# Two maxima of head 1 moved into the first section of scores, two of head 0 taken out of the second

## The chip, the cores and the metric

The kernel runs on one core of a Trainium2 chip. The time is the device time of one execution in microseconds (us); the figure for a kernel is the median of several runs. All views of the profile come from one profiled execution. PE is TensorE, PEld its weight loads, DVE VectorE, ACT ScalarE, POOL GpSimd, SP SyncE (which here issues almost all DMAs).

## The reference

Two mixers of a sequence of 2048 rows by 512 columns are computed and mixed row by row with a gate.

```python
def reference(A_x, A_dft_seq_re, A_dft_seq_im, A_dft_hid_re, A_dft_hid_im, B_x, B_wqkv, B_wo, gate_w):
    x = A_x                                                # both mixers read A_x
    g = sigmoid((x * gate_w).sum(-1, keepdims=True))
    # mixer A: real part of a DFT over the hidden, then over the sequence dimension
    a = einsum("bsd,ed->bse", x, dft_hid_re)
    b = einsum("bsd,ed->bse", x, dft_hid_im)
    y = einsum("ts,bse->bte", dft_seq_re, a) - einsum("ts,bse->bte", dft_seq_im, b)
    # mixer B: softmax attention, 32 heads of 16 columns, no mask
    q, k, v = heads(x @ wqkv)
    p = softmax(einsum("bhqd,bhkd->bhqk", q, k) * 16 ** -0.5)
    o = merge(einsum("bhqk,bhkd->bhqd", p, v)) @ wo
    return g * y + (1 - g) * o
```

All is float32. The kernel splits factors into a high and a low part and adds three products for each.

## The kernel before, in words

**Stages.** From 0 to about 195 us the kernel makes q and k of all heads and writes them to DRAM (`qk_d`), then v and the imaginary part of the hidden DFT. From 195 us on one stream of PE work runs to the end. Into it are woven the DFT products (`d`, line 471), the scores with their exponentials (`s`, lines 800 and 801), the row maxima that the softmax needs ahead of the scores (`a`, matmul at line 294, maximum over 512 columns by DVE at line 296), and the products of the exponentials with v (`acc`, line 846).

**Heads and pairs.** The 32 heads go as 16 pairs; of each pair head 0 works on rows 0 to 63 of the PE array and head 1 on rows 64 to 127. A pair's q and k lie in `qs[p % 2]` and `ks[p % 2]`, so that two pairs have room. `load_stacks(p, [h])` (lines 267 to 281) fills the 64 rows of head h from DRAM: one or two DMAs of constants and six of 128 KB, by turns q (line 280) and k (line 281), all issued by SP. The last of the six is a `ks<-qk`. For pair p it is called for head 0 at unit 32(p - 1) and for head 1 two units later:

```python
    for p in range(1, NP):
        for h in range(2):
            at(32 * (p - 1) + 2 * h * (p > 1), load_stacks, p, [h])
```

A unit is 128 keys by 1024 queries of both heads; 32 units make a pair. The scores of pair p begin at unit 32p.

**Maxima.** A head's maxima are a stream of its own: tile i of head h belongs to pair i // 64 (`a_tile`, lines 288 to 301). 44 tiles of each head are done before 195 us (`LEAD`). When both heads have done 32 tiles of a half pair, `m_parts` and `m_rows` (lines 303 to 326) form the negated maxima and send them to two rows of `qs`.

**Segments.** What stands in which order is written out by hand, as strings. `segment(pattern, half, ds, stop)` (lines 954 to 1003) goes through the slots of one. A slot of one letter issues one DFT product on the 64 rows of `half`, and beside it one score (`s`) or one maximum (`a`) of the other head, `1 - half`, on the other 64 rows; the two run side by side. `-` is a DFT product with nothing beside it. Two letters (`sA`, `aS`) are a score or maximum of the other head beside one, in capitals, of the head on `half`, with no DFT product. `+s` and `+a` are a score or a maximum with nothing beside it. A digit names the PSUM bank; without one, scores take turns on banks 0 to 2 and maxima on banks 3 to 5. `|` takes the next unit's products with v.

The stream is: 12 full-height DFT products (`pump`), `START[0]` on half 0, 12 more, `START[1]` on half 1, two units' products with v; then 13 times the two segments of `THIN`, 96 times two segments of `FULL`, 13 times the two of `NINE`, and a tail. In `THIN` a segment serves the other head with 7 maxima and the own one with 1. In `FULL` a segment on half 0 has 8 maxima of head 1, and the next, on half 1, 8 of head 0. The last four maxima of a `FULL` segment stand in its slots `a6 a3 a4 a1`, the last slot before `|`.

```python
    FULL = "a5 s4 a2 s0 a3 s6 a5 s4 s1 s0 s2 a6 a3 a4 s5 a1 | |"
    START = "sA s aS - - a s - - a s - - a", "s a s a s a s a s a s a +s +a"
    THIN = ("a2S4 a1 s3 a0 s6 s2 a4 s3 s1 a6 a0 s5 a2 s4A3 | |",
```

Each engine takes its instructions in order; a matmul that waits for data holds up all PE work behind it. SP, too, issues its DMAs in order.

Of the kernel before, what the change touches and what calls it, by code (L numbers as in the profile page):

```python
# [31 lines left out]
def mix_kernel(ctx: ExitStack, tc: tile.TileContext, xa_t, xa, wqkv, w_hid, w_seq, wo, gate_w, out):  # L32
# [820 lines left out]
    def take(gen, n, whole=True):  # L853

        got = []
        while len(got) < n:
            x = next(gen, None)
            if x is None:
                break
            x[0].left -= 1  # L860
            got.append((*x, x[0].left == 0))
            if whole and got[-1][4]:
                break
        return got
# [8 lines left out]
    def pump(gen, n):  # L873
        for x in take(gen, n, False):
            issue(x, None)
# [45 lines left out]


    FULL = "a5 s4 a2 s0 a3 s6 a5 s4 s1 s0 s2 a6 a3 a4 s5 a1 | |"
    START = "sA s aS - - a s - - a s - - a", "s a s a s a s a s a s a +s +a"
    THIN = ("a2S4 a1 s3 a0 s6 s2 a4 s3 s1 a6 a0 s5 a2 s4A3 | |",
            "a2S4 a1 s3 a0 s6 s2 a4 s3 s1 a6 a0 s5 a2 s4A3 | |")
    NINE = ("a3 s0 s5 a4 a1 s6 s3 a0 a2 s5A4 | s5S1 a3A0 |",
# [20 lines left out]
    def values(close=False):  # L948
        nonlocal valued
        i = pv(valued, close)  # L950
        valued += 1
        return i
# [69 lines left out]
    ds = take(hid, 12)  # L1022
    segment(START[0], 0, ds, False)
    pump(hid, 12)
    segment(START[1], 1, ds, True)
    values()
# [114 lines left out]
```

## Time and profile before

| | |
|---|---|
| time, median of 3 runs | 1656.97 us (1656.69 to 1657.71) |
| the profiled execution | 1657.73 us, its span 1656.0 us |
| PE busy | 1648.4 us, 100% of the span |
| DVE busy | 1381.0 us, 83% |
| ACT busy | 1259.6 us, 76% |
| POOL busy | 654.0 us, 39% |
| granted PE clock | 0.999 |

Busy times count overlapping instructions of an engine once. The time lies 1.73 us above the span of the same execution: what lies around the span is not in the views. In the views that list instructions the first number is the start in us from the span's start and the second the duration in us; SPq is SP's queue of DMA issues. A busy PE can still be waiting at the array's input, since the ends of its matmuls are modelled, so that starts are the safer reading.

### The profile page before, as it was taken

To read this page: it belongs to the slowest core of one execution; us is meant where nothing else is said; L and a number is where in the kernel's file an instruction comes from. 1 tells how busy PE (TensorE), PEld (TensorE's weight loads), DVE (VectorE), ACT (ScalarE), POOL (GpSimd) and SP (SyncE) were. 2 spreads that over 40 slices of the span, in tenths; PEclk is the share of its full clock that TensorE was granted. 3 is DMA by queue.
4 is the path that set the end of the run, shared out by engine and by line. 5 is a ranking of instruction groups with operands and counts; after the bars stand their busy time and mean duration, and the time that the engine had idled before them with its cause. 6 is when DMAs were issued, how large, how long until landed. Compare 5 with 4: busy or idle time off the path is not lost.

```text
span 1656.0 us, 34484 instructions
## 1 busy us (share of the span) xinstructions
PE 1648.4 (100%) x13082; PEld 990.4 (60%) x13082; DVE 1381.0 (83%) x2362; ACT 1259.6 (76%) x2469; POOL 654.0 (39%) x619
## 2 busy tenths in 40 slices
PE   9999999999999999999999999999999999999998
PEld 7888765555555555555555555555555555544454
DVE  5439888888888888888888888888888888899954
ACT  5212388888888888888788887888888887889996
POOL 0202133443434455444343455544434455333330
PEclk9999999999999999999999999999999999999999
DMA  9973610514151443414157434315141535452014
GB/s 291 348 166 109 186 20 9 70 34 85 46 91 47 74 113 81 95 46 79 47 90 255 92 115 95 87 59 92 47 91 56 116 104 119 139 186 47 25 44 142
DMA packets 85246, 167.16 MB, mean 101 GB/s; under 512 B 22460, under 2 KB 22716, under 8 KB 81068
## 3 DMA queue, kind: packets, MB, share of 16 engines
q1 hardware_dynamic: 84648, 164.30, 39.8%
q8 instruction: 103, 1.69, 0.5%
q10 hardware_dynamic: 432, 0.66, 0.1%
q14 instruction: 63, 0.52, 0.1%
HBM read 109.67 MB, written 55.17 MB: 100 GB/s over the span
## 4 chain that ended last, share of the span: by engine, by line
PE 99%; DMA 0%; DVE 0%; DVEq 0%; ACT 0%; SPq 0%; issue 0%
PE acc L846 28%; PE a L294 22%; PE s L800 19%; PE d L471 12%; PE s L385 3%; PE acc L800 3%; PE acc L294 2%; PE s L417 1%; PE d L385 1%; PE acc L808 1%; PE a L111 1%; PE a L110 1%; PE s L111 1%; PE s L110 1%; PE a L109 1%; PE s L109 1%
## 5 line engine op out<-in xcount | busy, mean ns | idle before, releaser
L296 DVE TENSOR_REDUCE mx<-a 128x1 f32<-128x512 f32 x1808 | 1127.8, 683 | 157.5 <-PE a L294 107.5
L801 ACT ACTIVATE pt<-s 128x512 f32<-128x512 f32 x1792 | 943.9, 628 | 15.1 <-PE s L800 11.1
L294 PE MATMUL a<-ks,qs 64*128 64x512 f32 (+1 forms) x1808 | 673.0, 408 | 0.0
L471 PE MATMUL d<-xab,ch 64*128 64x512 f32 x2016 | 648.1, 396 | 0.0
L800 PE MATMUL s<-qs,ks 64*128 64x512 f32 (+1 forms) x1792 | 591.5, 399 | 0.0
L828 POOL TENSOR_TENSOR oe<-oe,part 128x512 f32<-128x512 f32 x215 | 278.1, 1293 | 659.3 <-ACT part L827 654.3
L846 PE MATMUL acc<-pt,vt 128*17 128x512 f32 x3968 | 479.0, 595 | 0.0
L294 PEld LDWEIGHTS a<-ks,qs 64*128 64x128 f32 (+1 forms) x1808 | 322.2, 184 | 242.6 <-issue 133.1
L471 PE MATMUL d<-xab,cl 64*128 64x512 f32 x1008 | 399.3, 396 | 0.0
L471 PEld LDWEIGHTS d<-xab,ch 64*128 64x128 f32 x2016 | 366.6, 184 | 14.2
L800 PEld LDWEIGHTS s<-qs,ks 64*128 64x128 f32 (+1 forms) x1792 | 320.3, 184 | 81.0 <-ACT pt L801 29.8
L827 ACT COPY part<-acc 128x512 f32<-128x512 f32 x215 | 126.3, 588 | 202.2 <-issue 187.1
L846 PEld LDWEIGHTS acc<-pt,vt 128*17 128x17 f32 x3968 | 89.0, 96 | 228.2 <-issue 148.4
L471 PEld LDWEIGHTS d<-xab,cl 64*128 64x128 f32 x1008 | 185.6, 184 | 6.9
L296 DVE TENSOR_REDUCE mx<-acc 128x1 f32<-128x512 f32 x240 | 165.5, 690 | 11.4
L456 POOL TENSOR_TENSOR cl<-craw,ch 128x512 fp32r<-128x512 f32 x126 | 162.1, 1287 | 10.1
L801 ACT ACTIVATE pt<-acc 128x512 f32<-128x512 f32 x244 | 148.1, 607 | 0.0
L800 PE MATMUL acc<-qs,ks 64*128 64x512 f32 (+1 forms) x244 | 95.4, 391 | 0.0
L294 PE MATMUL acc<-ks,qs 64*128 64x512 f32 (+1 forms) x240 | 94.1, 392 | 0.0
L455 POOL CAST ch<-craw 128x512 fp32r<-128x512 f32 x126 | 77.1, 612 | 18.5 <-PE d L471 14.2
L471 PE MATMUL d<-wre,xab 64*128 64x512 f32 x336 | 83.0, 392 | 0.0
L471 PE MATMUL d<-wo_hl,o_hl 64*128 64x512 f32 x252 | 66.7, 395 | 0.0
(175 smaller groups left out, 1199.4 us busy)
## 6 DMA issues: line engine op xcount, KB each, us to landing
craw<-w_seq SPq DMA_DIRECT2D x128, 256.0 KB
qk<-hl SPq DMA_DIRECT2D x32, 512.0 KB
qs<-qk SPq DMA_DIRECT2D x96, 128.0 KB
ks<-qk SPq DMA_DIRECT2D x96, 128.0 KB
b<-hl SPq DMA_DIRECT2D x16, 512.0 KB
xab<-b SPq DMA_DIRECT2D x16, 512.0 KB
o<-oe SPq DMA_DIRECT2D x62, 128.0 KB
oh<-nh SPq DMA_DIRECT2D x12, 512.0 KB
```

The lines of the kernel that those rows point to most:

```text
L109: nc.tensor.matmul(ps, sh, mh, start=first, stop=False)
L294: nc.tensor.matmul(ps, qs[p % 2][r, qt * P:(qt + 1) * P], ks[p % 2][r, kb * 512:(kb + 1) * 512], start=True, stop=True)
L296: user = nc.vector.tensor_reduce(mx[p % 2][:, h, qt, kb:kb + 1], ps, AX.X, ALU.max)
L385: i = nc.tensor.matmul(ps, st[r], mv[r], start=not half and not j, stop=half == 1 and j == 11)
L455: nc.gpsimd.tensor_copy(h1, raw)
L456: nc.gpsimd.tensor_tensor(l1, raw, h1.bitcast(F32), ALU.subtract)
L471: i = nc.tensor.matmul(self.ps, st[r], mv[r], start=not self.begun, stop=stop)
L800: nc.tensor.matmul(ps, ks[p % 2][rr, kt * P:(kt + 1) * P], qs[p % 2][rr, q0:q0 + 512], start=True, stop=True)
L801: return nc.scalar.activation(pts[u][:, 2 * qb + h], ps, AF.Exp, bias=0.0, scale=DH ** -0.5)
L827: nc.scalar.copy(part[0], acc)
L828: nc.gpsimd.tensor_tensor(total, total, part[0], ALU.add)
L846: i = nc.tensor.matmul(acc[32 * j:32 * j + 17], v[:, 16 * h:16 * h + 17], pt[:, j], start=begin, stop=done or close)
```

## The change

Only the two strings of `START` change.

```diff
-    START = "sA s aS - - a s - - a s - - a", "s a s a s a s a s a s a +s +a"
+    START = "sA s aS a - a s a - s a - - a", "s a s a s a s a s a s s"
```

The first section has 14 slots as before, with six maxima of head 1 where it had four (and one score a slot earlier). The second has 12 slots where it had 14, with five maxima of head 0 where it had seven; its last score stands beside the last DFT product. The counts of scores, of DFT products and of all maxima stay. What changes for good is where the two streams of maxima stand: behind the two sections head 0 was at tile 52 and head 1 at tile 48; now both are at 50. All later patterns are the same, so at every later slot for a maximum, head 1 takes the tile two further on than before and head 0 the tile two further back, to the end.

PE in the first section, where `qs_973` and `ks_975` are the buffers of pair 0 and `d` is the DFT product; one piece of the difference:

```order
 L800 MATMUL s<-qs_973,ks_975 128x512
 L471 MATMUL d<-wre_1450,xab_204 128x512
+L294 MATMUL a<-ks_975,qs_973 128x512
 L471 MATMUL d<-wre_1451,xab_204 128x512
 L471 MATMUL d<-wre_1455,xab_204 128x512
-L294 MATMUL a<-ks_975,qs_973 128x512
+L800 MATMUL s<-qs_973,ks_975 128x512
 L471 MATMUL d<-wre_1451,xab_204 128x512
-L800 MATMUL s<-qs_973,ks_975 128x512
+L294 MATMUL a<-ks_975,qs_973 128x512
 L471 MATMUL d<-wre_1452,xab_204 128x512
 L471 MATMUL d<-wre_1456,xab_204 128x512
```

A maximum now stands beside a product that had nothing beside it, and the score and the maximum behind it have moved up.

PE at the end of the second section, up to the products with v (`acc<-pt,vt`):

```order
 L800 MATMUL s<-qs_973,ks_975 128x512
 L471 MATMUL d<-wre_1452,xab_204 128x512
-L294 MATMUL a<-ks_975,qs_973 128x512
-L800 MATMUL s<-qs_973,ks_975 128x512
-L294 MATMUL a<-ks_975,qs_973 128x512
+L800 MATMUL s<-qs_973,ks_975 128x512
 L846 MATMUL acc<-pt,vt 17x512 x8
```

Two maxima of head 0 are gone, and no score or maximum is left without a partner.

PE at the end of one `FULL` segment on half 0, the one in which head 1 goes over to pair 6 in the changed kernel; before, with the semaphores that each instruction waits for (`qs_974`, `ks_976` hold pair 5, and `qs_973`, `ks_975` pair 6; DMAHW are those of SP's DMAs):

```order
L294 MATMUL a<-ks_976,qs_974 128x512 [waits DVE_49]
L471 MATMUL d<-xab_206,ch 128x512
L294 MATMUL a<-ks_976,qs_974 128x512 [waits Activation_49]
L471 MATMUL d<-xab_206,cl 128x512
L800 MATMUL s<-qs_974,ks_976 128x512 [waits DVE_49]
L471 MATMUL d<-xab_206,ch 128x512 x2
L294 MATMUL a<-ks_976,qs_974 128x512 [waits Activation_49]
L846 MATMUL acc<-pt,vt 17x512 [waits DVE_49]
```

and after:

```order
L294 MATMUL a<-ks_976,qs_974 128x512 [waits DVE_49]
L471 MATMUL d<-xab_206,ch 128x512
L294 MATMUL a<-ks_975,qs_973 128x512 [waits DMAHW3_49,DMAHW4_49,DMAHW2_49,DMAHW5_49,DMAHW1_49,DMAHW6_49,DMAHW0_49,Activation_49]
L471 MATMUL d<-xab_206,cl 128x512
L800 MATMUL s<-qs_974,ks_976 128x512 [waits DVE_49]
L471 MATMUL d<-xab_206,ch 128x512 x2
L294 MATMUL a<-ks_975,qs_973 128x512 [waits Activation_49]
L846 MATMUL acc<-pt,vt 17x512 [waits DVE_49]
```

The last two maxima of head 1 in this segment read the new pair's buffers, and the first of them waits for the DMAs that fill head 1's rows. Before, the first instruction of head 1 with such a wait is the first maximum of the next segment on half 0, 42 instructions further on. The orders of ACT and of SP are unchanged by the whole edit.

## The prediction

> **What bounds the kernel now.** I read the page first, its busy times and the engines of the chain that ended last.
>
> ```profile
> span 1656.0 us, 34484 instructions
> ...
> PE 1648.4 (100%) x13082; PEld 990.4 (60%) x13082; DVE 1381.0 (83%) x2362; ACT 1259.6 (76%) x2469; POOL 654.0 (39%) x619
> ...
> PE 99%; DMA 0%; DVE 0%; DVEq 0%; ACT 0%; SPq 0%; issue 0%
> ```
>
> PE is busy for the whole span and carries 99% of the chain. No DMA is on the chain: every load lands before PE asks for it. So a slot less on PE shortens the kernel, and a wait of PE lengthens it, unless PE has slack behind it. For that I read the chain in order of time, in the stretch of three `FULL` segments.
>
> ```profile
> 671.00 1.84 PE acc L846 x16
> ...
> 676.73 1.84 PE acc L846 x16
> ...
> 682.47 1.84 PE acc L846 x16
> ```
>
> A segment takes 5.73 to 5.74 us, of which 1.84 are products with v. Single slots follow from the timeline of PE in the same place:
>
> ```profile
> 675.86 0.39 PE L294 MATMUL a<-ks,qs 64*128 64x512 f32 x1
> ...
> 676.33 0.39 PE L294 MATMUL a<-ks,qs 64*128 64x512 f32 x1
> ...
> 676.66 1.91 PE L846 MATMUL acc<-pt,vt 128*17 128x512 f32 x16
> ...
> 684.25 0.49 PE L294 MATMUL a<-ks,qs 64*128 64x512 f32 x1
> ```
>
> Slots `a4`, `s5`, `a1` of a segment on half 0: two slots take 0.47 us, so one takes 0.23 to 0.24, all through. PE runs at its own pace there, not at that of DVE or ACT. What it loses in a wait it cannot win back.
>
> The last row is the first maximum of head 1 in pair 6 before the change (the first of its segment). Changed, pair 6 begins for head 1 at the slot of 675.86, 8.39 us earlier. So I looked at when the loads land. The timeline of SP, for the same pair:
>
> ```profile
> 659.05 0.39 SPq L274 DMA_DIRECT2D qs<-z  x1
> ...
> 661.70 0.42 SPq L281 DMA_DIRECT2D ks<-qk  x1
> ...
> 665.50 0.42 SPq L274 DMA_DIRECT2D qs<-z  x1
> ```
>
> Head 0's seven loads are issued from 659.05 to 661.70, head 1's from 665.50, and the last of these at 669.77 (its row is below). The views give no landing times, so I read the share of time that the DMA engines are busy, in windows of 1 us (the last two numbers of a row are that share and GB/s):
>
> ```profile
> 676.00:677.00 1.00, 1.00 (x12) 0.41 (x12) 1.00 (x2) 1.00 (x4) 0.00 (x0) 1.00 1.03 111
> 677.00:678.00 1.00, 1.00 (x16) 0.24 (x8) 1.00 (x3) 0.56 (x2) 0.00 (x0) 1.00 0.74 129
> 678.00:679.00 1.00, 1.00 (x12) 0.46 (x6) 0.31 (x1) 0.30 (x1) 0.00 (x0) 1.00 0.06 20
> ...
> 314.00:315.00 1.00, 1.00 (x11) 0.70 (x10) 1.00 (x3) 1.00 (x3) 0.82 (x1) 1.00 0.30 84
> 315.00:316.00 1.00, 1.00 (x12) 0.93 (x9) 1.00 (x3) 1.00 (x3) 0.00 (x0) 1.00 0.00 0
> ```
>
> At 676 all sixteen engines are still busy; on average they are done at 677.74, and the last shortly after 678. That is 8.0 us behind the issue of the last load on average, and some 8.2 to 8.7 for the last packet. The windows at 315 say the same of pair 2, whose last load is issued at 306.35: done on average at 314.30, 7.95 us behind it, and wholly before 315, 8.65 behind. I take 8.2 us from the last issue to the landing, an estimate from these two places, and 7.9 to 8.7 as its bounds. For pair 6 that gives a landing at 677.97: 6.3 us before its use now, 2.1 us after its use in the changed kernel.
>
> **The change part by part.** *The landing.* The issue of the last load of head 1, for pairs 2 to 14:
>
> ```profile
> 306.35 0.30 SPq L281 DMA_DIRECT2D ks<-qk  x1
> 393.52 0.30 SPq L281 DMA_DIRECT2D ks<-qk  x1
> 484.41 0.30 SPq L281 DMA_DIRECT2D ks<-qk  x1
> 576.26 0.30 SPq L281 DMA_DIRECT2D ks<-qk  x1
> 669.77 0.30 SPq L281 DMA_DIRECT2D ks<-qk  x1
> 760.24 0.30 SPq L281 DMA_DIRECT2D ks<-qk  x1
> 851.89 0.30 SPq L281 DMA_DIRECT2D ks<-qk  x1
> 945.27 0.30 SPq L281 DMA_DIRECT2D ks<-qk  x1
> 1036.17 0.30 SPq L281 DMA_DIRECT2D ks<-qk  x1
> 1127.62 0.30 SPq L281 DMA_DIRECT2D ks<-qk  x1
> 1220.82 0.30 SPq L281 DMA_DIRECT2D ks<-qk  x1
> 1310.76 0.30 SPq L281 DMA_DIRECT2D ks<-qk  x1
> 1403.26 0.30 SPq L281 DMA_DIRECT2D ks<-qk  x1
> ```
>
> and the slots that will need them, at pair 2 (in `THIN`, its last `a2`; the row merges two maxima) and at the first and last of the twelve in `FULL`:
>
> ```profile
> 310.18 0.67 PE L294 MATMUL a<-ks,qs 64*128 64x512 f32 x2
> ...
> 400.36 0.39 PE L294 MATMUL a<-ks,qs 64*128 64x512 f32 x1
> ...
> 1410.57 0.39 PE L294 MATMUL a<-ks,qs 64*128 64x512 f32 x1
> ```
>
> The places come from counting. Head 1 now enters `THIN` at tile 50 and gains 8 a pair of segments, so tile 128 is the seventh maximum of a half-0 segment; it enters `FULL` at 154, so every pair begins at the seventh maximum of such a segment, slot `a4`. Eleven pairs lie between 400.36 and 1410.57, 91.84 us each; I place the slots between by that period. From last issue to slot that leaves, for pairs 2 to 14: 3.83, 6.84, 7.79, 7.78, 6.11, 7.48, 7.67, 6.13, 7.07, 7.46, 6.10, 8.00 and 7.31 us. Taken from 8.2, the waits are 4.37, 1.36, 0.41, 0.42, 2.09, 0.72, 0.53, 2.07, 1.13, 0.74, 2.10, 0.20 and 0.89 us: 17.0 us together. With 7.9 they make 13.2, with 8.7 23.5.
>
> Queued behind each wait is all PE work: the DFT products, the scores, and through them ACT and DVE. Nothing covers it. The loads' own issue does not move against PE: it follows the last scores of the pair before last, so that a wait at one pair shifts the next pair's loads and uses together.
>
> *The restart.* A weight load that is hidden beside a running matmul is bare after a wait:
>
> ```profile
> L294 PEld LDWEIGHTS a<-ks,qs 64*128 64x128 f32 (+1 forms) x1808 | 322.2, 184 | 242.6 <-issue 133.1
> ```
>
> 184 ns, so 0.2 us a wait and 2.6 us for 13; bounds 0 and 4.3, the latter with 0.33 us, the step from 676.33 to 676.66 in which PE changes from 64-row products to those with v.
>
> [...]
>
> *The first two sections.* PE and DVE there, before:
>
> ```profile
> 204.85 0.40 PE L800 MATMUL s<-qs,ks 50*128 50x512 f32 x1
> 205.11 0.50 PE L294 MATMUL a<-ks,qs 48*128 48x512 f32 x1
> 205.54 1.91 PE L846 MATMUL acc<-pt,vt 128*17 128x512 f32 x16
> ...
> 202.57 4.28 DVE L296 TENSOR_REDUCE mx<-a 128x1 f32<-128x512 f32 x7 [2.88 <-PE a L294]
> ```
>
> The two lone matmuls and the step to the products with v take 0.69 us, from 204.85; with the last score beside the last DFT product only a step like that of 0.33 us stays, at about the place of the lone score's start less one slot, so some 0.6 us go. Against it, the first section has seven maxima in 14 slots: seven reductions take 4.28 us, 0.61 each, and the slots 14 times 0.24, 3.4 us. The maxima share three banks, so the last of them, and the full-height chain that takes the bank after them, may wait; at most for the 0.9 us by which DVE is behind. DVE was idle for 2.88 us before the second section, which covers the rest. I take a gain of 0.3, with bounds of a gain of 0.6 and a loss of 0.3.
>
> *The rest.* Head 0's uses come later, which costs nothing. For pairs 1 and 15 the new use lies over 5 us behind the landing by the same count. In `NINE` the negated maxima are made up to one segment earlier and in the last segment four maxima change places; PE waits for neither now. I count zero, 0.3 us either way.
>
> *Sum.* 17.0 + 2.6 - 0.3 = 19.3 us. The profiled execution takes 1657.73 us (1656.0 of span and 1.73 around it), which gives 1677.0; it is 0.76 above the median of 1656.97, so for the median I say 1676.3. A measurement of this kernel can tell about 0.2%, 3.3 us, from no change; the sum is six times that.
>
> **The rivals.**
>
> *The loads are there in time.* This one is not slower. If head 1's loads land 4.4 us sooner than I have it, no slot waits, and the first sections alone remain: 1656.97 - 0.3 = 1656.7. For all pairs but 2 it decides at a landing 6.1 us behind the last issue, for pair 2 at 3.8. Against it stand the windows at 676 to 678, with every engine busy past the slot. 6%.
>
> *PE wins part of it back.* If the 5.74 us of a segment were set by DVE (eight reductions of 0.61, 4.9 us) or ACT, work stored up during a wait would let PE run faster afterwards. If half came back, 9.7 would stay: 1656.97 + 9.7 = 1666.7. Against it: the slots' even 0.23 us. 9%.
>
> *More is lost.* The landing takes 8.7 us and the restart 0.33: 23.5 + 4.3 - 0.3 = 27.5, or 1684.5. For it: the last packets are behind the average, and a wait ends with the last. 6%.
>
> *The clock falls.* If PE's clock halves after the longest wait, 4.4 us at pair 2, and stays so for as long as 14 slots, these take 3.4 us more: 1679.7. Against it: the granted clock is 1.00 in all windows above, but none holds a wait. 10%. The Trainium skill (TensorE: Matmul & The Clock Gate, Part 1) has the clock halve after about 3.4 us of idling and return after about 3.4 us of work; by it only pair 2 is at risk, for an estimate of 1.7 us more.
>
> **How the numbers follow.** The forecast has 69%, the rivals 6, 9, 6 and 10. The likeliest time is 1676.3. The range runs from 1667, which takes in part of the half that comes back and the lower bound of the landing with restart (13.2 + 0 - 0.3, 1669.9), to 1684, just short of the upper bound. Slower by over 0.2% has 94%; of the 6% with no wait, 4 lie within 0.2% and 2, with more gained at the start or in the tail than I see, below it.
>
> **What would show it.** In the changed profile the chain would name DMAs (`ks<-qk`) at the slot `a4`, and PE's waits would list them, 13 times, longest at pair 2 with about 4.5 us; those of pairs 6, 9 and 12 near 2.2. The segments with these slots would take 5.74 us plus the wait, all others 5.74 as before, and the products with v behind `START` would begin some 0.3 us earlier, near 205.2. I am wrong if segments at the pairs' changes keep 5.74 us, if PE waits there for something other than loads, or if time is lost in segments without a change of pair.

## The result, and the profile after

The changed kernel takes 1684.88 us (median of 4 runs, 1680.13 to 1686.64) against 1657.13 us: a ratio of 1.0162 (95% interval 1.015 to 1.0173), 27.8 us slower. Its profiled execution took 1686.64 us. Page and chain:

```profile
span 1684.9 us, 34427 instructions
...
PE 1658.8 (98%) x13082; PEld 988.8 (59%) x13082; DVE 1381.0 (82%) x2362; ACT 1260.8 (75%) x2469; POOL 654.8 (39%) x619
...
PE 91%; DMA 5%; issue 1%; ACT 1%; POOL 1%; SPq 0%; DVE 0%; DVEq 0%; POOLq 0%
```

The span is 28.9 us longer. DVE, ACT and POOL do the same work; DMA is now on the chain. The timeline of PE has these rows with idle time before them (in brackets, with the releaser the view infers), from 200 us to the tail:

```profile
314.03 0.80 PE L294 MATMUL a<-ks,qs 64*128 64x512 f32 x2 [4.28 <-DMA craw<-w_seq]
...
408.56 0.46 PE L294 MATMUL a<-ks,qs 64*128 64x512 f32 x1 [1.93 <-ACT pt L801]
...
500.92 0.46 PE L294 MATMUL a<-ks,qs 64*128 64x512 f32 x1 [0.32 <-DMA ks<-qk]
...
687.71 0.76 PE L294 MATMUL a<-ks,qs 64*128 64x512 f32 x1 [2.66 <-DMA ks<-qk]
...
783.59 0.46 PE L294 MATMUL a<-ks,qs 64*128 64x512 f32 x1 [0.90 <-ACT pt L801]
...
875.85 0.46 PE L294 MATMUL a<-ks,qs 64*128 64x512 f32 x1 [0.22 <-ACT pt L801]
...
969.85 0.46 PE L294 MATMUL a<-ks,qs 64*128 64x512 f32 x1 [1.94 <-DMA no<-r]
...
1064.89 0.46 PE L294 MATMUL a<-ks,qs 64*128 64x512 f32 x1 [1.40 <-ACT pt L801]
...
1157.86 0.47 PE L294 MATMUL a<-ks,qs 64*128 64x512 f32 x1 [0.86 <-ACT pt L801]
...
1252.20 0.46 PE L294 MATMUL a<-ks,qs 64*128 64x512 f32 x1 [2.21 <-DMA ks<-qk]
...
1439.23 0.47 PE L294 MATMUL a<-ks,qs 64*128 64x512 f32 x1 [1.52 <-DMA ks<-qk]
```

Eleven waits, 18.2 us, each in front of head 1's first maximum of a pair: 2, 3, 4, 6 to 12 and 14. The releasers' names should not be trusted: the view infers them, and a wait for several semaphores is put down to the one that came last. `craw<-w_seq` and `no<-r` share semaphores with the loads. The exponentials named five times had ended 0.2 to 0.9 us before the maximum started; at pair 3, where it started at 408.56, the row of ACT ends at 407.65. What points to the cause is the place, and the time since the issue of the last load. Those two rows, pair 3's exponentials and pair 6's last load:

```profile
405.57 2.08 ACT L801 ACTIVATE pt<-s 128x512 f32<-128x512 f32 x4
...
678.72 0.30 SPq L281 DMA_DIRECT2D ks<-qk  x1
```

From the issue at 678.72 to the maximum at 687.71 are 8.99 us. Over the eleven waits this time is 8.0 to 9.1 us, 8.6 on average. That it is the loads and not ACT is shown below, where the loads alone are exchanged.

That leaves over 10 us. Windows of 3.4 us around two of the waits (pair 6, then pair 2; in each row the third number from the end is the granted PE clock):

```profile
683.80:687.20 3.40, 1.25 (x12) 0.69 (x8) 2.27 (x4) 2.26 (x5) 0.13 (x1) 0.99 0.87 115
687.20:690.60 3.40, 2.89 (x14) 1.21 (x18) 1.38 (x2) 0.60 (x1) 0.00 (x0) 0.50 0.02 5
690.60:694.00 3.40, 3.40 (x18) 1.14 (x12) 0.33 (x1) 0.59 (x1) 0.23 (x1) 0.50 0.00 0
694.00:697.40 3.40, 3.40 (x34) 2.52 (x34) 3.21 (x6) 3.31 (x7) 2.97 (x3) 1.00 0.00 0
...
311.70:315.10 3.40, 1.07 (x3) 0.50 (x3) 0.27 (x1) 0.00 (x0) 0.00 (x0) 0.50 0.45 69
315.10:318.50 3.40, 3.40 (x17) 0.49 (x16) 1.01 (x2) 0.60 (x1) 0.00 (x0) 0.50 0.00 0
```

The clock is halved behind the wait at pair 6 for two windows, and PE gets 18 matmuls through a full window instead of 34. It is halved behind pair 2, and for one window each behind pairs 9 and 12:

```profile
970.50:973.90 3.40, 3.40 (x20) 0.49 (x16) 1.24 (x2) 0.60 (x1) 0.00 (x0) 0.50 0.21 78
...
1253.80:1257.20 3.40, 3.40 (x18) 1.16 (x12) 0.51 (x2) 0.59 (x1) 0.24 (x1) 0.50 0.00 0
```

PE works at half clock for 4.5 us (from 314.03 to 318.5), 6.3 (2.89 + 3.40), 3.4 and 3.4. Half of that, 8.8 us, is lost, if all work of PE takes twice as long at half clock; this is an estimate.

The first two sections, from the first paired slot to the products with v; the first row is the kernel before (its products with v start at 205.54), the others the changed one:

```profile
195.44 0.50 PE L800 MATMUL s<-qs,ks 50*128 50x512 f32 x1
...
195.19 0.50 PE L800 MATMUL s<-qs,ks 50*128 50x512 f32 x1
...
198.89 3.01 PE L471 MATMUL a<-wre,xab 128*128 128x512 f32 x12
...
204.98 1.48 PE L846 MATMUL acc<-pt,vt 128*17 128x512 f32 x12
```

9.79 us, where it was 10.10: a gain of 0.31. So the 28.9 us are 18.2 of waits and 8.8 of clock, less 0.3; the remaining 2.2 are left over for the restarts.

The starts of the products with v, set against those of before, give these parts one by one. At the seven waits behind which the clock stayed at 1.00 the segment is 0.2 to 0.3 us longer than its wait explains. Pair 5's is 0.35 us longer, though the list above has no row for it. At pairs 2, 6, 9 and 12 the loss beyond the waits is 9.3 us together; less 0.25 for each, 8.3 are left for the clock. With the 0.3 us gained these parts make 29.3, and this execution came to the first section 0.25 us earlier, so that the 28.9 are accounted for to about 0.1 us. Around the wait at pair 3:

```profile
406.24 0.39 PE L294 MATMUL a<-ks,qs 64*128 64x512 f32 x1
408.56 0.46 PE L294 MATMUL a<-ks,qs 64*128 64x512 f32 x1 [1.93 <-ACT pt L801]
408.86 0.39 PE L800 MATMUL s<-qs,ks 64*128 64x512 f32 x1
```

Idle time is counted from the end of the matmul before, 0.39 us behind its start, while without a wait the next would have started 0.23 us behind it. So 0.16 us of each of these remainders belong to the wait, and only about 0.1 is a restart.

### The profile page after: what moved, and what is told of

It is laid out like the page before. It is cut to its first block, busy times and chain, and to the rows that moved or that the text cites. A ratio compares the mean times of both kernels' runs of the same rounds, so it can differ in the third digit from the quotient of the medians.

```text
span 1684.9 us, 34427 instructions
## 1 busy us (share of the span) xinstructions
PE 1658.8 (98%) x13082; PEld 988.8 (59%) x13082; DVE 1381.0 (82%) x2362; ACT 1260.8 (75%) x2469; POOL 654.8 (39%) x619
## 4 chain that ended last, share of the span: by engine, by line
PE 91%; DMA 5%; issue 1%; ACT 1%; POOL 1%; SPq 0%; DVE 0%; DVEq 0%; POOLq 0%
PE acc L846 26%; PE a L294 21%; PE s L800 18%; PE d L471 10%; PE s L385 3%; PE acc L800 2%; DMA ks<-qk 2%; PE acc L294 2%; DMA craw<-w_seq 1%; PE s L417 1%; PE acc L808 1%; PE d L385 1%; PE a L110 1%; PE a L109 1%; PE s L110 1%
## 5 line engine op out<-in xcount | busy, mean ns | idle before, releaser
L846 PE MATMUL acc<-pt,vt 128*17 128x512 f32 x3968 | 484.9, 602 | 0.0
```

The source lines that it names most:

```text
L846: i = nc.tensor.matmul(acc[32 * j:32 * j + 17], v[:, 16 * h:16 * h + 17], pt[:, j], start=begin, stop=done or close)
```

## The experiments

**One part alone.** The first section changed, the second left as it was (head 1 at tile 50, head 0 at 52):

```diff
-    START = "sA s aS - - a s - - a s - - a", "s a s a s a s a s a s a +s +a"
+    START = "sA s aS a - a s a - s a - - a", "s a s a s a s a s a s a +s +a"
```

> Only the first section is changed; the second keeps its seven maxima of head 0 and its lone score and maximum, so head 1 stands at tile 50 and head 0 at 52. Theory (head 1 goes over to a new pair before its loads have landed): the same waits as in the changed kernel, between 0.2 and 4.3 us at pairs 2 to 14, with PE's clock halved behind the longest; about 1685 us (1680 to 1688). Rival (the loss comes from the shorter second section or from head 0 being two tiles back): near 1657.

Measured: 1687.05 us, ratio 1.0176 (1.0162 to 1.019). PE's waits in its profile:

```profile
PE a L294 <- DMA ks<-qk: 6.9, 4, 2.6
PE a L294 <- ACT pt L801: 5.6, 5, 2.0
PE a L294 <- DMA craw<-w_seq: 4.4, 1, 4.4
PE a L294 <- DMA no<-r: 2.0, 1, 2.0
```

Eleven waits again, 18.9 us. The whole loss comes with head 1's two tiles, and the shorter second section has no part in it.

The second section alone (head 1 at tile 48, head 0 at 50):

```diff
-    START = "sA s aS - - a s - - a s - - a", "s a s a s a s a s a s a +s +a"
+    START = "sA s aS - - a s - - a s - - a", "s a s a s a s a s a s s"
```

> Only the second section is changed; the first is the old one, so head 1 stays at tile 48 and head 0 is at 50. Theory: no wait for a load anywhere, and the products with v behind the two sections start about 0.6 us earlier: 1656.5 us (1656.0 to 1656.9), a little faster than before. Rival: 1670 to 1685.

Measured: 1656.87 us against 1657.42, ratio 0.9997 (0.9988 to 1.0006). The expected gain is within the interval, and so is none. In its profile the sections do get shorter:

```profile
194.95 0.50 PE L800 MATMUL s<-qs,ks 50*128 50x512 f32 x1
...
204.46 1.05 PE L846 MATMUL acc<-pt,vt 128*17 128x512 f32 x8
```

9.51 us instead of 10.10, with no wait of PE for a load. It is the best version seen, by a margin that the runs cannot tell from zero.

**The same order on PE, the loads earlier.** The changed kernel with the two heads' loads exchanged:

```diff
-            at(32 * (p - 1) + 2 * h * (p > 1), load_stacks, p, [h])
+            at(32 * (p - 1) + 2 * (1 - h) * (p > 1), load_stacks, p, [h])
```

> The changed kernel, with the two heads' loads of pairs 2 to 15 exchanged: head 1's at unit 32(p - 1), head 0's two units later. PE's order is that of the changed kernel. Theory: head 1's loads land some 6 us earlier and no slot waits for them; head 0's land just in time, with at most 0.3 us at pair 2: 1656.7 us (1656.2 to 1657.5). Rival (the new order on PE, DVE or POOL costs the time): 1685 as in the changed kernel.

Measured: 1657.59 us, ratio 1.0000 (0.9991 to 1.0009). The median is 0.09 us above the expected range, the interval holds the expected value. PE's order is the changed one and all of the loss is gone; from 200 us to the tail no row of PE has a wait before it, neither for a load nor for ACT. The chain of this kernel's page:

```profile
PE 99%; DMA 0%; DVE 0%; DVEq 0%; ACT 0%; issue 0%; SPq 0%
```

DMA is off it. The last load of those that are now head 1's, for pair 6, in the timeline of SP:

```profile
661.95 0.42 SPq L281 DMA_DIRECT2D ks<-qk  x1
```

It is issued at 661.95 instead of 669.77. This settles the cause of the waits: the maxima of head 1 overtook the landing of their operands.

**Half the shift.** One maximum more in the first section, one fewer in the second (head 1 at tile 49):

```diff
-    START = "sA s aS - - a s - - a s - - a", "s a s a s a s a s a s a +s +a"
+    START = "sA s aS a - a s - - a s - - a", "s a s a s a s a s a s a +s"
```

> Half the shift: the first section has one maximum of head 1 more than before, the second one of head 0 fewer, so head 1 stands at tile 49 and head 0 at 51. Theory: head 1 goes over in FULL in the last slot of the segment (a1), 0.47 us later than in the changed kernel, and in THIN one segment later. No wait at pair 2; the others 0.47 us shorter, 9.7 us together, with 1.6 for restarts and 2 to 4 for the clock: about 1670 us (1667 to 1675). Rival (only a shift of two tiles goes over a limit): near 1657.

Measured: 1671.78 us, ratio 1.0087 (1.0073 to 1.0101). The waits are seven, and none at pair 2; the two largest, in the timeline of PE:

```profile
680.05 0.46 PE L294 MATMUL a<-ks,qs 64*128 64x512 f32 x1 [1.86 <-DMA ks<-qk]
...
1238.81 0.47 PE L294 MATMUL a<-ks,qs 64*128 64x512 f32 x1 [1.98 <-DMA ks<-qk]
```

and the window behind the one at pair 6:

```profile
681.60:685.00 3.40, 3.40 (x18) 1.66 (x12) 1.06 (x2) 1.18 (x2) 1.13 (x1) 0.50 0.00 0
```

Together 8.0 us where 9.7 were expected; the clock fell once. Already one tile moves the pair's first maximum into the segment before, and costs 14.4 us. The second tile adds the rest of the loss: 0.2 to 0.8 us on each of these seven waits, the wait at pair 2 and those at pairs 4, 8 and 11, and three more falls of the clock.

**The clock.** The changed kernel with matmuls whose results are overwritten, in front of the maxima that wait:

```diff
         r = slice(64 * h, 64 * h + (64 if p else 48))
+        if h and not j:
+            q_t, k_t, r0 = qs[1 - p % 2], ks[1 - p % 2], slice(64, 112)
+            for _ in range({2: 17, 3: 7, 6: 10, 7: 3, 9: 7, 10: 5, 11: 3, 12: 8, 14: 5}.get(p, 0)):
+                nc.tensor.matmul(ps, q_t[r0, :P], k_t[r0, :512], start=True, stop=True)
         nc.tensor.matmul(ps, qs[p % 2][r, ...
```

> The changed kernel with idle matmuls (their results are overwritten) in front of head 1's first maximum of pairs 2, 3, 6, 7, 9, 10, 11, 12 and 14: 17, 7, 10, 3, 7, 5, 3, 8 and 5 of them, about 0.23 us each and each a little less than the wait there. Theory (the waits cost about 18 us, and a clock that halves because PE stands idle costs 7 to 10 more): PE isn't idle, the clock stays at 1.00, and the loads land when they land: 1676 us (1673 to 1679), faster than the changed kernel though it has 65 matmuls more. Rival (the clock does not follow idling): 1685. Rival (the waits are no waits for landings, and the matmuls come on top): 1700.

and beside it the changed kernel once more:

> The changed kernel once more, beside the other two. Theory: waits at the same pairs within 0.5 us, but another set of pairs with a halved clock, since the clock's steps seem to follow a grid of 3.4 us of its own: 1680 to 1688 us. Rival (the clock falls at the same pairs each time): pairs 2, 6, 9 and 12 again.

Measured: 1681.62 us filled and 1684.68 us again (ratios to before 1.015, 1.0135 to 1.0165, and 1.0163, 1.0148 to 1.0178). With 65 matmuls more the median is 3 us lower, a third of the gain that was expected; the intervals overlap, so the times alone do not show a gain. The profile of the filled kernel says why. Its timeline of PE at pair 6 (line 297 is the added one), then SP's issue of the last load and the wait at pair 9:

```profile
682.40 2.45 PE L297 MATMUL a<-ks,qs 48*128 48x512 f32 x10
685.11 0.46 PE L298 MATMUL a<-ks,qs 64*128 64x512 f32 x1 [0.26 <-DMA ks<-qk]
...
956.22 0.82 SPq L281 DMA_DIRECT2D ks<-qk  x1
...
965.78 0.46 PE L298 MATMUL a<-ks,qs 64*128 64x512 f32 x1 [1.84 <-DMA rc<-o]
```

The window behind the wait at pair 6, and the two at pair 9:

```profile
685.40:688.80 3.40, 3.40 (x30) 1.42 (x29) 1.71 (x3) 1.35 (x3) 0.02 (x1) 1.00 0.00 0
...
963.70:967.10 3.40, 1.56 (x12) 0.68 (x14) 0.81 (x2) 0.58 (x1) 0.00 (x0) 1.00 0.66 171
967.10:970.50 3.40, 3.40 (x20) 0.89 (x14) 0.47 (x1) 0.43 (x2) 0.00 (x0) 0.50 0.03 5
```

Where the filling covered the wait (pair 6, also 2 and 12), the clock stayed at 1.00. At pair 9 PE idled for 1.84 us in spite of seven added matmuls, and the clock fell: in this execution the maximum started 9.6 us after the issue of its last load, where it was 8.3 in the changed kernel. By the starts of the products with v, pairs 2, 6 and 12 lost 4.9, 2.8 and 2.7 us here and 6.7, 5.9 and 4.1 in the changed kernel, while pair 9 lost 5.4 instead of 3.8. So the clock follows PE's idling; what it takes is read from profiles (8.3 to 8.8 us, and here 1.7), and the medians show it only in part. In the run again the clock fell behind pairs 2, 6, 9 and 12, the same as before, which was the rival's mark; but in the kernel with the first section alone it fell behind 2, 6, 10 and 12.

**Later loads that were not later.** The kernel before, with head 1's loads called four units behind head 0's instead of two:

```diff
-            at(32 * (p - 1) + 2 * h * (p > 1), load_stacks, p, [h])
+            at(32 * (p - 1) + 4 * h * (p > 1), load_stacks, p, [h])
```

> The kernel before, with head 1's loads called four units behind head 0's instead of two, one segment later; PE's order is that of before. Theory: landings 5.5 to 5.7 us later. Pair 2's then comes at about 320.5, 2.4 us behind its use at 318.2; pair 6's at about 684.4, 0.2 behind; the others just in time. With restarts and some clock 3 to 6 us: 1661 us (1659 to 1664). Rival (only the place of the maxima on PE matters): 1657.

Measured: 1657.7 us, ratio 1.0001 (0.9991 to 1.001): a miss. The last loads of pairs 6 and 9 in SP's timeline:

```profile
670.24 0.30 SPq L281 DMA_DIRECT2D ks<-qk  x1
...
952.10 0.42 SPq L281 DMA_DIRECT2D ks<-qk  x1
```

Pair 6's is issued at 670.24 instead of 669.77; only those of pairs 5, 9 and 13 come 6 to 7 us later (952.10 instead of 945.27), and they had over 6 us to spare. Pair 9's was just in time; its first maximum in this kernel starts 8.2 us behind the issue, without a wait:

```profile
960.27 0.50 PE L294 MATMUL a<-ks,qs 64*128 64x512 f32 x1
```

A place one segment later, 5.74 us of PE's time, moved ten of the thirteen issues by at most 0.8 us. I read this as SP running ahead of PE, so that a later place in SP's order delays a load only by the waits that it is moved past; that is inferred. No run has these loads really late under the old order on PE.

## Why the prediction was right, and where it was short

- *Direction and cause: right.* Slower, at the changes of pair, in front of head 1's first maximum, through the landing of its loads. With the loads exchanged, the loss is gone under the same order on PE.
- *The waits: right in place, short in size.* 17.0 us were forecast, and the rows show 18.2; pair by pair for 2, 3, 6, 9, 12 and 14, 4.37 / 4.28, 1.36 / 1.93, 2.09 / 2.66, 2.07 / 1.94, 2.10 / 2.21 and 0.89 / 1.52. The forecast counted from the slot's own start; counted so, the eleven waits are 20.0 us, as each row leaves out 0.16. Pairs 5 and 13, forecast at 0.42 and 0.20, have no wait over 0.2. The 8.2 us from issue to landing were too low: up to the start of the maximum it is 8.6 on average, and four of the eleven times lie above my bound of 8.7. I had read the mean end of the engines' work, and the wait ends with the last.
- *Restart and first sections.* 2.6 us were forecast for restarts, about 0.1 us each is seen; that the cause is the bare weight load is not shown. Waits and restarts together were forecast at 19.6 and measured at 21.3. A gain of 0.3 in the sections was forecast, 0.31 measured.
- *The clock: the step that was left out of the sum.* It stood among the rivals at 10%, for pair 2 alone, at 3.4 us. It happened at four waits of 1.94 us and more and took 8.3 to 8.8 us. That is most of the 9.6 us by which the span's 28.9 exceed the sum's 19.3, and it puts the measured 1684.88 just above the upper end of the range, 1684. One of my signs of being wrong did appear by it: the segments behind these four waits lose time without a change of pair. My reason, that no window of before showed a lower clock, was empty, as none of those windows held an idle PE. The rule that I cited (the Trainium skill, TensorE: Matmul & The Clock Gate, Part 1) gave the right mechanism; read as "about 3.4 us of idling" it left out the waits near 2 us, which the trace shows to be enough.
- *The rival of time won back: wrong.* After each wait the segments go on at their old pace or slower.
- *The rival of more loss: near by luck.* Its 1684.5 is close to the 1684.88 measured, but it has 27.8 us of waits and restarts and no clock. Measured were 21.3 us of these, and the clock made up the difference.

## What to carry to other kernels

An instruction moved ahead by a few slots can cross the landing of a load that it never waited for. So for every stream that a change shifts, look up its next operand load and compare the use with the landing, not with the issue. In a kernel that runs PE without a pause, price a wait with the clock that may fall behind it: here 18 us of waits brought over 8 us of half clock with them.

## What the runs showed of the hardware

The clock's low stretches start and end on a grid of 3.4 us that runs on its own (311.7, 687.2, 970.5 and 1253.8 in the changed kernel lie 110, 83 and 83 steps of 3.413 us apart). In a window at full clock, what fits all the waits of these profiles is how long PE idles within that window. 1.78 us and more halved the clock in the next one; 1.63 and less did not. The two nearest cases come from two other executions (the window with the wait, then the next one; first the kernel with the first section alone, then the changed kernel again):

```profile
1061.40:1064.80 3.40, 1.62 (x14) 0.68 (x14) 2.15 (x5) 1.91 (x4) 1.27 (x2) 0.99 0.96 278
1064.80:1068.20 3.40, 3.40 (x18) 0.81 (x12) 0.56 (x1) 0.10 (x1) 0.00 (x0) 0.50 0.01 2
```

```profile
1436.50:1439.90 3.40, 1.77 (x16) 0.73 (x16) 2.29 (x5) 2.06 (x5) 0.00 (x0) 1.00 0.30 51
1439.90:1443.30 3.40, 3.40 (x32) 1.85 (x26) 1.93 (x4) 1.79 (x5) 1.02 (x1) 1.00 0.00 0
```

In a window at half clock less was enough to keep it there: pair 6's window from 687.2 has 0.51 us of idle time, and the next is at 0.50 too. With no idle time, as behind pairs 9 and 12, the clock came back after one window.

A wait of 1.93 us that fell across a border of the grid (at 407.3 us in the changed kernel) left the clock at 1.00, and one of 1.94 us inside a window halved it. The runs of the changed kernel lie up to 6.5 us apart (1680.13 to 1686.64); how the waits fall on the grid may be the reason, which no profile of the faster ones shows.
